# A hand-written order of 1,064 tasks, replaced by another one: split attention and a gated feed-forward block on one core

## The chip, the core and the metric

The kernel runs on one core of one Trainium2 chip. The core has five engines with a queue each: TensorE (PE, with its weight loads shown apart as PEld), VectorE (DVE), ScalarE (ACT), GpSimd (POOL) and SyncE (SP), which in this kernel does nothing but issue transfers. An engine takes its instructions strictly in the order in which they are written; an instruction whose input isn't ready holds up all behind it. The metric is the device time of one execution in microseconds.

## The reference

Four batches (B = 4) of eight heads, 768 positions, 64 numbers per head. Heads 0, 2 and 6 attend causally to all positions. The other five ("streams") see only the first 4 positions and a causal window of 64. The attention's output, laid out as 3072 rows of 512, goes through a gated feed-forward block.

```python
# cut to the core
scores = scale * np.matmul(q, k.transpose(0, 1, 3, 2))
stream_keep = causal & (is_sink | in_win)
mask = np.where(retr[0, :, 0, 0, None, None], full_mask, stream_mask)
a = np.exp(scores - max); a = a / (np.sum(a) + 1e-09); attn = np.matmul(a, v)
x = attn.transpose(0, 2, 1, 3).reshape(B * S, H * D)          # 3072 x 512
g = x @ w_gate                                                # 512 x 1536
out = (g * sigmoid(g) * (x @ w_val)) @ w_out                  # 1536 x 512
```

## The kernel before

**Tiles and tasks.** The sequence is cut into 24 tiles of 128 positions (numbered 0 to 23) in 12 pairs (q0 to q11, k0 to k11 and x0 to x11 are the loads of a pair's q, k and v). Four tiles make a group of 512 rows for the feed-forward block, so there are six groups (g0 to g5). All the work is written as 1,064 tasks, and each is a small function with a name. A name carries its tile or group. The ones that the text speaks of are these:

- `load q3` and the like (L341): a transfer from memory issued by SP into one of 11 raw buffers; a load has to wait until the casts from the buffer's last user are done. `cq`, `ck` (L429) cast q and k to fp16, `cx` (L446) casts v into the table `vt`, `wc g`, `wc v`, `wc o` (L376) cast the weights. For these ACT uses L206, POOL L208 and DVE L212.
- `trq`, `trk` (L469): eight transposes on TensorE for the pairs 0 to 4; `evq`, `evk` (L475) copy them to SBUF. For later pairs SP issues a transposing transfer instead, `dq`, `dk` (L462).
- `sc` (L551, matmuls at L567): scores of a tile in up to four units, each into two PSUM banks. `ex` (L569, L579): the exponential on ACT. `mask` (L581, L587): a product with a mask, on DVE or POOL. `val` (L591, L597): scores times values. `nm` (L600): reciprocal and scaling on DVE, which writes `xb`. `sk`, `sv` (L495, L502): copies of the first four keys and values into each tile's block.
- `xtr` (L609) with `xe` (L624): transposes of a tile's result on TensorE, for tiles 0 to 7; for later ones SP issues `xdma`.
- `gate` and `vals` (L755, matmuls at L759): four matmuls of 512 columns each for one of 12 blocks of the hidden layer; in g0 the blocks 0 to 3 come in halves of 256 columns. `tanh` (L763) on ACT, `stt1` and `stt2` (L767, L773) on DVE.
- The output projection of g0 to g4 uses seven products in place of eight (`out0.p1` to `p7`, L830, matmuls at L839), on sums of blocks of the hidden layer (`hs`, L818, L826) and of the weights (`ws`, L408, L412), each on DVE or POOL. `oe` (L850, L855) gathers the products on DVE or ACT, and `st` (L857) stores them. g5 uses plain matmuls (`out5`, L788, L793).
- `warm` (L315, L321): matmuls that compute nothing. There are ten at the start, and some more groups of fillers between the first transposes.

**What sets the order.** There is no scheduler in the program. Three tables hold what an offline planner chose. `ORDER` is a string of two-digit numbers, the sequence in which the tasks are written into the engines' queues; numbers from 3700 up are warm-ups. `WAYS` has one digit for each task: which of its allowed engines runs it. `SLOTS` has one digit for each buffer taken: which buffer of a ring, and which of the eight PSUM banks. Dependencies are not in the tables; a task's instructions wait by semaphores for what they read and for the former users of their buffers and banks.

```python
for number in P.order():
    if number < P.FILL:
        running.append(P.tasks[number])
        P.tasks[number].run()
    else:
        warm((number - P.FILL) % 16, (number - P.FILL) // 16)
```

Of the kernel before, what the change touches and what calls it, by code (L numbers as in the profile page):

```python
# [13 lines left out]


ORDER = (
    "060004071W1U1V1X0103xz1c1d1ey01f1gzI1i1j092021280A22232B052C2D021hyU1p1q1r1s292A2E2F2L2M0D2X2f2g"
    "2h081Y1b1Z1a1k1l1m1t1u1v0C2W2c2d2e2N2O2S1w2l2m0B24252G2H2I27262P2Q1n2J1o2R1y1z1x2i2j2t2K0F3C3I3J"
    "3K0g0z8o8p0y8e8f8q2U2o2p30310m108h2V8t8j8k8m2k2n8g8i8u8v2x382y0h0E2a2Y118w8x8r8s8l8n13939D9E9F98"
    "999A8y8z902Z2q2r2u2s3334940G3D3L0n14919B9C9596979G9H923M3R3N3S3W3X0k0i161C9h9i9j9c9d9e2z3U3V320H"  # L20
    "3H3G3F3E3O3b9N9O9P9I9J2b353P3637390q1D9f9g9K9k9l3T0o3i3j3f3g179Q9L9R9M3Q3Y3Z3a3c0l1F9r9s9t9m9n9o"
    "3n3o0I3u3l3m0j199S9T9U9X9Y0J3v4344453h3p2v2w3A3B3d3e3k3q3r400p1A9V9W9Z0r1G9p9q4149424A4B464H4748"
    "9u9v9zA13s3t0S0t150N4b4a0M9a9b9yA04N4O4Q4RATB9BABBB4B5B6B7B8BEBFBG0L4P0ZBCBDAd0w1E1M1N1P1O4K4L4M"
    "4C4DAQARASAUAaAbAcAeAfAgAh0x0v0s12ApAqAr4dAO0K3y3z3w3xALAMAiAjANAP0u18BH0XAVAWAX0P0R6vAzB00YB2AY"
    "AZB1B30W1B1K1I4Z4h4gAkAlAmAuAv2T4E4F4Y4e4f0O1H1S1Q1R1T1J1L9wA29xA30c4G4J5D5K5L4I5f5lBIAwA4A6A7A5"
    "ACAA4V4l4m4n4i4j4kA8A9ABADAnAo4v4y4z51505C5I5JAEBMAGAKAF4S4T4U4W4X52AsAtAxAyBLBN0T4q4r4o4p535g5n"
    "5o54AHAIAJBO4s4t4u554w4xBJBPBK56575j5T6KBQ5W5cBX5X5Y4c58596x5A7Q5B7T6z7R707SBZBRBSBTBU5U5VBVBWBY"
    "Ba5s5t5u0a0Q5G5E5F5H5M715N725OBvBsBtBuBwBiBjBk0U6H6JCMCNCOCbCcCd0e81CPCQCWCXCYBlBm5v5w5i5p5q605Z"
    "5a5b5dCeCfCCCDCE5m6364696A6566CHCICJ5rCRCSCFCGCT0V6I6PBxBy5k6y6N5P5Q5R5S67CKCLBz6w73BnBoCACUCVBp"
    "5h5x5y5z62BbBcBdBh68C7C8C2C3616B6C6F6DBqBrC9CBCiCkC4CZCaC0C174BeBf6E6X6YC5C6CjCl6G6U6R6S6M6e6Z6a"  # L30
    "6V6W5eDoDjDkDlDpDqDUDVDWDtDuDrDsDvDADBDwDxDCDmDn0b7P7X7W7O7U6T6b6c6d6fCgCmCh757677Bg7F7G7H7C7L7D"
    "7EDXDYD5D6D788DPDQDRDKDLDDDEDMD8D96L6ODyDzE07I7J7K6gE1E2CnCsCt6Q6h6i6n6o6j6k6l6mDSDT78797A7BDFDG"
    "DHDeDfDg7b7c7d6p6q7Y7j7Z7aDIDJDhDi6r6s6tDZDaDbCoCrCqCp7M7e7f7V7p7q7r7mDNDODcDd7n7o7N6uEmEpEnFLFM"
    "FNFGFHFIFJEcEdEo0d80867g7h7i7k7l8789CuCvEqCyCzE6E8EeCwCxD0D4D1D2D3FKE5E7Ez7x8A8I8J8D8E8F8NFOFP8B"
    "FEFBFCFDFFEwExEyF0EkErEsEtEhEiEjElEuEvE3EAE4E97s7t0f8582838G8WF1F2F3EBEE7u7v7w7z8X8H7yEC8CEFEG8Y"
    "8Z8T8QEX8K8U8L8R8O8M8PEa84F9EYEZF6F7EV8VEHEIEJEK8S8a8b8c8dEfEDEOEbF8FAESETEUEWELENEREMEPEQFTFVGO"
    "GPGQGWGTGUG7GMGCEgGVGXG9GAGBGDGiGjGkGRGSGJGKGLGNGYGZGaGEGFF4F5FpFqFrGHGbGcGGGIGdGeGfFuFvFsFzG0Fx"
    "G2FtFwFyFQFRFXGgGhGlGmG4G5G6FgFYFZG1G3FSFUFeFiFWFaFcG8GnGoGpFbFlFdFfFhFkFoGsGtGuGxFjFmFnGqGrGvGw"
    "GyGzH2H3H0H1H4H7H5H6H8H9"
)  # L40
WAYS = (
    "000010000000000000000000000000000000000000000000000000000000222202201212222202221010000011102210"
    "112200100100000010000000110121212222011000000000000000002100220212011000000000000000200001001000"
    "000201221100011000001001000000000010010010000000011210200010000000000000002000100100000220200110"
    "000000100000000002000010000000000000222200000010000001001000220002020000000100100000010001001000"
    "002102020020000001000000000012000100100000000000110000000000000010000002000001000000001001000001"
    "100000000000022002122100000000000000000100001001000000000000000000000000000000000000000000000000"
    "000000000000000000000000000000000000000000001101000000000000000000000000000000000000000000000000"
    "000000000000000000000000000000001011100010000000000000000000000000000000000000000000000000000000"
    "000000000000000000001010010011000000000000000000000000000000000000000000000000000000000000000000"  # L50
    "000000000110100001000000000000010000000000000000000000000000000000000000000000000000000000000010"
    "111000000000000000001000000000000000000000000000000000000000000000000000000000000000000000000000"
    "00000010"
)
SLOTS = (
    "0015237641826A24867A334524510096788A3905049A38374311A0210016040006142212230223221646560314104140"
    "626231644345614020144616220605456340646213420426144610636540602041626520626443414041046062165222"
    "032434461616520426242614563246106325444261114060612262132061636012442636230612042456120412463601"
    "110301420002121011020041003512510202113212010230020110200131100103213000013001410101124002510051"
    "104021200020030110412312301000011101031025103501111141014010011221012012230001011134102101001021"  # L60
    "500141102110102001101122000430014120110135300021000202140124125310000110110510451041000201004201"
    "4510104111200301151124210311034100202040001001202430120"
)
DIGITS = "0123456789ABCDEFGHIJKLMNOPQRSTUVWXYZabcdefghijklmnopqrstuvwxyz"

# [954 lines left out]
```

## Time and profile before

| | us |
|---|---|
| runs | 248.15, 248.54, 248.74 (median 248.54) |
| the profiled execution | 248.22 |
| its span, first to last instruction | 246.1 |
| TensorE busy | 234.8 |
| VectorE busy | 190.5 |
| ScalarE busy | 148.5 |
| GpSimd busy | 132.7 |

The span is what the profile sees; the execution's own time has about 2.1 us more around it. TensorE's granted clock is full in every slice. Matmuls overlap: the profile gives the time of one from start to end, and in a run of them the next starts earlier than that, so the spacing between starts, and not the mean duration, tells what a series costs. The same holds in a smaller measure for the other engines, whose queued instructions overlap by some 0.05 to 0.1 us.

Transfers: in the first 64 us the loads of 512 KB land one after another, about 1.5 us apart; after that SP mostly waits for the task whose result it is to move.

### The profile page before, as it was taken

The page shows a single profiled execution, that of the slowest core. Times are in us where ns is not written, and L with a number is a line of the kernel's source. Part 1 is how long each engine was busy: PE and PEld are TensorE (multiplying, and loading weights), DVE is VectorE, ACT ScalarE, POOL GpSimd, SP SyncE. Part 2 cuts the span into 40 slices and gives each one's busy share as a digit, 9 for nine tenths or more (in the row PEclk, how much of TensorE's full clock was granted, in tenths as well). Part 3 has the DMA queues.
Part 4 walks back from the last instruction along what each step waited for, and adds up shares of the span by engine and source line. Part 5 has one row for each costly group of instructions (what it writes and reads, how often), then busy time and mean ns, then how long its engine had stood idle before and what let it go on. Part 6 is the DMA issues. An engine that isn't in the chain of part 4 may idle for free.

```text
span 246.1 us, 5624 instructions
## 1 busy us (share of the span) xinstructions
PE 234.8 (95%) x2191; PEld 143.6 (58%) x2191; DVE 190.5 (77%) x326; ACT 148.5 (60%) x236; POOL 132.7 (54%) x137
## 2 busy tenths in 40 slices
PE   7989999999997998999998998999999999999994
PEld 2667755644456777545653645648457664456752
DVE  0769989899998997785889876788698588876920
ACT  5698798877975779869527875653547303321011
POOL 7688697907894585989574063844510802132000
PEclk9999999999999999999999999999999999999999
DMA  6999999999579979992483381632731114000044
GB/s 188 357 346 339 334 353 351 312 310 352 141 221 170 244 159 239 212 243 67 87 164 85 55 159 23 87 86 47 211 92 21 24 21 170 3 0 0 3 170 170
DMA packets 66793, 40.72 MB, mean 165 GB/s; under 512 B 25168, under 2 KB 60240, under 8 KB 66768
## 3 DMA queue, kind: packets, MB, share of 16 engines
q1 hardware_dynamic: 66224, 39.33, 61.8%
q10 hardware_dynamic: 544, 1.05, 1.1%
q8 instruction: 17, 0.28, 0.5%
q14 instruction: 8, 0.07, 0.1%
HBM read 28.31 MB, written 6.29 MB: 141 GB/s over the span
## 4 chain that ended last, share of the span: by engine, by line
PE 75%; DVE 11%; POOL 4%; DMA 3%; issue 3%; SPq 2%; ACT 1%; POOLq 0%; DVEq 0%; ACTq 0%
PE banks L759 38%; PE banks L839 16%; PE banks L567 7%; PE banks L597 5%; PE banks L793 4%; PE banks L321 3%; POOL wt_sb L412 2%; DMA qT<-hq 2%; DVE h_sb L775 2%; PE banks L473 2%; DVE sil L769 2%; DVE xb L605 1%; DVE wt_sb L412 1%; DMA kT<-hq 1%; DVE e L587 1%
## 5 line engine op out<-in xcount | busy, mean ns | idle before, releaser
L579 ACT ACTIVATE e<-banks 128x1024 f16<-128x1024 f32 (+2 forms) x68 | 59.0, 910 | 23.1 <-PE banks L567 15.3
L759 PE MATMUL banks<-xt,wv_sb 128*128 128x512 f16 (+1 forms) x304 | 71.1, 368 | 0.2 <-ACT e L579 0.2
L759 PE MATMUL banks<-xt,wg_sb 128*128 128x512 f16 (+1 forms) x304 | 69.5, 368 | 1.3 <-DVE h_sb L775 0.7
L765 ACT ACTIVATE sig<-banks 128x512 f32<-128x512 f32 (+1 forms) x76 | 43.0, 574 | 43.4 <-PE banks L759 30.2
L587 POOL TENSOR_TENSOR e<-e,m 128x1024 f16<-128x1024 f16 (+1 forms) x25 | 45.9, 1846 | 34.3 <-ACT e L579 34.1
L769 DVE SCALAR_TENSOR_TENSOR sil<-sig,banks 128x512 f32<-128x512 f32 (+1 forms) x76 | 49.2, 657 | 12.9 <-ACT sig L765 10.0
L775 DVE SCALAR_TENSOR_TENSOR h_sb<-sil,banks 128x512 f16<-128x512 f32 (+1 forms) x76 | 49.0, 655 | 5.5 <-PE banks L759 3.8
L759 PEld LDWEIGHTS <-wg_sb 128*128 128x128 f16 x304 | 28.8, 98 | 31.9 <-issue 2.2
L759 PEld LDWEIGHTS <-wv_sb 128*128 128x128 f16 x304 | 28.1, 98 | 29.3 <-issue 1.2
L839 PEld LDWEIGHTS <-h_sb 128*128 128x128 f16 x360 | 34.5, 98 | 8.2 <-DVE wt_sb L412 1.8
L855 DVE TENSOR_TENSOR out_sb<-banks,out_sb 128x512 f32<-128x512 f32 x35 | 23.7, 688 | 6.1 <-PE banks L839 5.5
L826 POOL TENSOR_TENSOR h_sb<-h_sb 128x768 f16<-128x768 f16 x11 | 18.7, 1704 | 15.3 <-DVE hs_sb L826 14.9
L839 PE MATMUL banks<-wt_sb,h_sb 128*128 128x256 f16 x180 | 21.8, 273 | 1.5 <-DVE wt_sb L412 1.5
L567 PE MATMUL banks<-qT,kT 64*128 64x128 f16 x472 | 20.3, 218 | 2.8 <-DVE qT L208 1.0
L839 PE MATMUL banks<-wo_sb,h_sb 128*128 128x256 f16 x180 | 21.9, 273 | 0.0
L567 PEld LDWEIGHTS <-kT 64*128 64x128 f16 x472 | 14.5, 94 | 12.3 <-issue 8.9
L597 PEld LDWEIGHTS <-e 128*128 128x128 f16 x472 | 17.1, 97 | 3.8 <-DVE out_sb L855 0.5
L206 ACT COPY out_sb<-banks 128x512 f32<-128x512 f32 (+1 forms) x9 | 5.1, 574 | 22.2 <-DMA out_dram<-out_sb 14.8
L597 PE MATMUL banks<-vt,e 128*128 128x65 f16 x472 | 18.0, 193 | 0.5 <-POOL vt L208 0.4
L208 POOL CAST vt<-raw 64x512 f16<-64x512 f32 x19 | 11.7, 615 | 10.7 <-DMA raw<-in_v_dram 10.2
L605 DVE TENSOR_TENSOR xb<-banks,rc 128x512 f16<-128x512 f32 x24 | 16.6, 692 | 0.9
L826 POOL TENSOR_TENSOR hs_sb<-h_sb 128x768 f16<-128x768 f16 x5 | 8.2, 1642 | 10.4 <-DVE h_sb L775 8.6
(60 smaller groups left out, 217.7 us busy)
## 6 DMA issues: line engine op xcount, KB each, us to landing
raw<-in_v_dram SPq DMA_DIRECT2D x12, 512.0 KB, 6.6
raw<-in_q_dram SPq DMA_DIRECT2D x8, 512.0 KB, 4.5
raw<-in_k_dram SPq DMA_DIRECT2D x8, 512.0 KB, 5.3
out_dram<-out_sb SPq DMA_DIRECT2D x8, 512.0 KB, 3.3
raw<-in_moe_w_gate_dram SPq DMA_DIRECT2D x6, 512.0 KB, 7.9
raw<-in_moe_w_val_dram SPq DMA_DIRECT2D x6, 512.0 KB, 8.5
raw<-in_moe_w_out_dram SPq DMA_DIRECT2D x6, 512.0 KB, 7.8
raw<-in_q_dram SPq DMA_DIRECT2D x8, 256.0 KB, 6.5
```

The lines of the kernel that those rows point to most:

```text
L567: nc.tensor.matmul(sc[:, c:c + n, :], weights, moving, start=first, stop=last)
L579: nc.scalar.activation(out=to, in_=src, func=AF.Exp, scale=scale)
L587: ENG[task().way].tensor_tensor(out=ev, in0=ev, in1=mm, op=ALU.mult)
L597: nc.tensor.matmul(avs[t][:, odd, n * 66:n * 66 + 65], ee, vv, start=(m == 0), stop=(m == len(bl) - 1))
L605: nc.vector.tensor_tensor(out=xb.rearrange("p n o d -> p o n d"), in0=av[:, :, :, 0:64], in1=rc.to_broadcast([128, 2, 4, 64]), op=ALU.mult)
L759: nc.tensor.matmul(ps, wsb[:, kk, j * 128:(j + 1) * 128], xt[:, kk, c[0]:c[1]], start=(kk == 0), stop=(kk == 3))
L765: nc.scalar.activation(out=sg[g, j, c], in_=gs[g, j, c], func=AF.Tanh, scale=0.5)
L769: nc.vector.scalar_tensor_tensor(out=sl[g, j, c], in0=sg.pop((g, j, c)), scalar=1.0, op0=ALU.add, in1=gs.pop((g, j, c)), op1=ALU.mult)
L775: nc.vector.scalar_tensor_tensor(out=hs[g, j][:, c[0]:c[1]], in0=sl.pop((g, j, c)), scalar=0.5, op0=ALU.mult, in1=vs.pop((g, j, c)), op1=A ...
L826: ENG[T_hs[g, x][part].way].tensor_tensor(out=to, in0=a, in1=b, op=op)
L839: nc.tensor.matmul(rooms[g, p][:, x], left[:, j, 128 * x:128 * x + 128], right[:, j], start=(j == 0), stop=(j == NK - 1))
L855: nc.vector.tensor_tensor(out=cell(*to), in0=rooms[g, p], in1=cell(*other), op=ALU.add)
```

## The change

Only the three tables change. The 1,064 tasks, what they compute, their dependencies, the buffers and the rings are the same. The plan before was made for one chip; the one after was made for the mean over four chips, with durations that were varied and with transfers that land later.

```diff
 ORDER = (
-    "060004071W1U1V1X0103xz1c1d1ey01f1gzI1i1j092021280A22232B052C2D021hyU1p1q1r1s292A2E2F2L2M0D2X2f2g"
...
-    "GyGzH2H3H0H1H4H7H5H6H8H9"
+    "0306071W091U1V1X000A08xy1c0D0C01050B1d1e040gy01f1gzJ1i1h2021282922232B1j1r1s021p1q1w0F2C2D2E2F1b"
...
+    "GzH0H2H3H4H5H7H1H6H8H9"
 )
 WAYS = (
-    "000010000000000000000000000000000000000000000000000000000000222202201212222202221010000011102210"
...
+    "000010000000000000000000000000000000000000000000000000000000221202202202212200200111000111110010"
...
 SLOTS = (
-    "0015237641826A24867A334524510096788A3905049A38374311A0210016040006142212230223221646560314104140"
...
+    "0014237653916A152371476981504A39A2564807049A28352A9168410016041002241601230163620442561014104122"
...
```

Read out, the tables differ in this:

- 120 tasks change their engine and 395 of the chosen buffers and banks are others. Warm-up groups: 3, 4, 4 and 2 before, 2, 4 and 5 after.
- Of the masks 13 ran on DVE and 25 on POOL, now 16 and 22; of the `ws` 7 and 5, now 4 and 8; the `hs` stay 19 and 21 in number, but are dealt otherwise. All `evq` but two go to ACT (two before), most `evk` and `xe` to DVE. Five of the `wc o` are on ACT (three before), none on POOL (two before). Four more stores are issued from ACT.

TensorE's queue up to the first feed-forward matmuls (W and a number: so many warm-ups):

```
before: warm W3 trq0 W4 trk0 W4 sc0.0 trq1 trk1 W2 sc1.0 sc1.1 sc2.0 sc3.0 trk2 val0 val1 trq2 sc3.1 sc4.1
        val2 val3 xtr0 xtr2 xtr1 sc4.0 trq3 gate0.1.0 gate0.0.0 xtr3 sc4.2 sc5.1 vals0.0.0 gate0.1.256
after:  warm W2 trq0 W4 trk0 W5 sc0.0 trq1 trk1 sc1.1 sc1.0 sc2.0 sc3.0 sc3.1 trk2 val1 val0 trq2 val2 sc4.1
        sc4.0 xtr0 xtr1 val3 sc5.1 xtr2 gate0.0.0 gate0.1.0 xtr3 sc4.2 trq3 gate0.1.256
```

ACT's and POOL's queues after, at the places that the text works through (before in brackets where it matters):

```
ACT:  cq0.0 cq0.1 ck0.1 evq0.0 evq0.1 mfill0 evq1.0 ex0.0 ex1.1 ex1.0 sk0.1 ex2.0 ex3.0 ex3.1 cx1.0.1 evq2.0
      evq2.1 ex4.1 ex4.0            [before: mfill0 ck0.1 evq0.0 evk0.0 ex0.0 evk1.0 evk1.1 ex1.0 ex1.1 ...]
POOL: wc g0.1 sk0.2 wc g0.0 mask4.1 mask4.0 wc v0.1 wc g1 ck3 wc v1 mask5.1 cx2.1.1 cx2.0.0 wc g4 mask5.0
      wc v4 mask6.1 sk0.4 wc g2 wc v2 mask6.0 cq4 wc g3 mask7.1 ck4
POOL: ws4.1 ws1.2 ws2.2 ws3.2 hs0.3.0 cx4.0.0 ws2.0 ws3.0 mask9.1 ws4.0 ws4.2 mask10.1 mask11.1 hs1.1.1 mask11.0
      [before: wc o3 ws3.0 ws1.0 sv1.1 cq5 wc o5 ws3.2 ws1.2 ws2.2 hs0.2.1 mask10.0 mask11.0 hs1.1.1 hs1.3.1]
POOL: ck10 hs2.3.0 hs2.2.0 mask20.1 mask19.1   beside DVE: stt1 3.10.0 hs2.2.1 nm16 stt1 3.5.0
```

SP's queue in the middle, after (the loads and transfers that stand behind a wait):

```
... dq6.0 dq6.1 dq7.0 st0.h1 dk7.0 load x10 st0.h0 xdma10 load q9 xdma11 xdma9 load k8 load x6 dk7.1 ...
... xdma13 dq8.0 xdma15 st1.h0 dq10.0 load k10 dk10.1 dk10.0 xdma16 load q11 ...
... dq11.0 xdma17 st2.h1 dk11.0 load x11 xdma20 xdma22 xdma21 xdma23 st3.h1 st5.2.0 st5.3.0 st5.3.1
```

## The prediction

> **What bounds the kernel now.** I read the page first, then the waits, then TensorE's timeline task by task. From the page, the span, the engines' shares and TensorE's row of slices:
>
> ```profile
> span 246.1 us, 5624 instructions
> ...
> PE 234.8 (95%) x2191; PEld 143.6 (58%) x2191; DVE 190.5 (77%) x326; ACT 148.5 (60%) x236; POOL 132.7 (54%) x137
> ...
> PE   7989999999997998999998998999999999999994
> PEclk9999999999999999999999999999999999999999
> ```
>
> TensorE (PE) is the bound: 95%, at full granted clock. The change leaves its work alone, so what can move is time in which it works below its rate. To see that, price its work at the spacing of back-to-back matmuls in the chain that ended last, for example:
>
> ```profile
> 193.78 2.62 PE banks L839 x24
> ...
> 201.59 18.99 PE banks L759 x88
> ```
>
> That is 109 ns for a 256-column matmul of a product and 216 ns for one of 512 columns. In the same way 128 columns take about 57, a score matmul 34, a value matmul 30 and a mark about 110. 544 gate/vals matmuls x 216 = 117.5, 64 short ones x 109 = 7.0, 420 in products x 109 = 45.8, the last output projection 10.4, 472 scores 16.0, 24 marks 2.6, 472 values 14.2, 112 transposes 6.4, 23 warm-ups 5.0: **224.8 us**. TensorE starts at 1.4 and its last matmul ends at 242.8, 3.3 before the end. So 246.1 = 1.4 + 224.8 + 16.6 + 3.3, and 16.6 us are lost inside. Setting each task's start against the running sum gives the places: 2.4 before the first transposes (warm-ups spaced 0.43 instead of 0.216), 4.2 between 6.6 and 32, 6.0 in eight stalls after 73, and about 4 in small steps, mostly 0.1 at each of the 30 turns into score matmuls. Only the 4.2 and the 6.0 belong to the plan.
>
> Three of the late stalls share a cause. The timeline around them (columns: start, us, engine, line, operation):
>
> ```profile
> 75.06 1.64 POOL L826 TENSOR_TENSOR h_sb<-hs_sb,h_sb 128x768 f16<-128x768 f16 x1
> 75.11 2.68 DVE L412 TENSOR_TENSOR wt_sb<-wo_sb,wt_sb 128x512 f16<-128x512 f16 x3 [0.70 <-POOL wt_sb L412]
> 77.84 0.83 PE L839 MATMUL banks<-wt_sb,h_sb 128*128 128x256 f16 x6 [1.55 <-DVE wt_sb L412]
> ...
> 88.92 1.97 POOL L826 TENSOR_TENSOR h_sb<-h_sb 128x768 f16<-128x768 f16 x1
> 89.42 1.88 DVE L826 TENSOR_TENSOR h_sb<-h_sb 128x768 f16<-128x768 f16 x1
> 93.20 0.62 PE L567 MATMUL banks<-qT,kT 64*128 64x128 f16 x16 [0.91 <-DVE xb L605]
> ...
> 130.36 2.12 POOL L587 TENSOR_TENSOR e<-e,m 128x1024 f16<-128x1024 f16 x1 [0.69 <-ACT e L579]
> 130.38 2.51 DVE L826 TENSOR_TENSOR h_sb<-h_sb 128x768 f16<-128x768 f16 x1
> ...
> 229.15 0.55 DVE L826 TENSOR_TENSOR h_sb<-h_sb 128x768 f16<-128x768 f16 x1
> ```
>
> A VectorE (DVE) sum of two SBUF operands takes 0.55 with GpSimd (POOL) idle and 1.88 or 2.51 beside a POOL operation. These blocks led to 1.7 lost at 77.8 (out0.p4), 1.1 at 93.2 (sc13.0) and 0.5 at 134.5 (gate3.1.0). The others: 0.6 at 108.5 (x6 landed at 105.7), 0.4 at 111.0 (dq7.1), 0.6 at 129.7 (a bank), 0.9 at 149.8 (dk8.1), 0.2 at 189.4.
>
> **The change part by part.** Total work per engine, from its mean intervals between queued operations: ACT 136.4 to 137.8, DVE 180.1 to 177.6, POOL 132.0 to 127.7. None nears TensorE, so this alone is worth nothing; only what ends a wait counts.
>
> *Warm-ups.* 13 fillers become 11: 2 x 0.216 = **-0.43**, if nothing else fills the hole.
>
> *Opening, by hand from landings and durations of before.* Loads land about 1.5 us apart and the first four keep their places. q0 is cast on ACT (5.1 to 6.25), the 12 warm-ups end at 1.36 + 12 x 0.427 = 6.5, and sc0.0 starts at 9.34 against 9.22 (five fillers before it instead of four). mfill0 (2.25 on ACT, in cover at 4.3 before) now stands behind evq0.1: ACT is free again at 10.5, ex0.0 ends at 12.2, ex1.1 at 13.1, ex1.0 at 14.05, ex2.0 at 15.3, ex3.0 at 16.2. Banks hang on these, so sc3.1 loses 0.2 and val0.1 0.4; val2.1 waits for cx1.0.1 on ACT until 17.7 (0.75). In exchange evk1, evk2, xe0 and xe1 moved to DVE, and sc4.1, which lost 1.05 to DVE's evq2, starts at 18.2, after val2. gate0.0.0 starts at 20.2 (21.7 before), gate0.1.256 waits for v0's cast and xe3 until 22.6, trk3 ends near 28.5. Lost since the first transposes: 3.0 to 3.3 against 4.2. I take **-0.9**; bounds -1.6 and +0.5, for landings that shift by one place (1.5).
>
> *POOL from 19 to 46.* It now has sk0.2, mask4.0, mask4.1 and sk0.4 among its casts. At sc7.0 TensorE has done 29.2 us of its work and needs POOL's first 29.3; before, 31.2 and 27.4: 3.9 us of lead gone. Chained: cx2.0.0 ends at 29.7, then g4 30.75, mask5.0 32.85, v4 33.9, mask6.1 35.3, sk0.4 35.75, g2 36.8, v2 37.8, mask6.0 39.9, g3 42.0. sc7.1, gate0.4.0 and trq4 want their inputs at 35.7, 36.8 and 41.2: no slack. I take **+0.4**; bounds 0 and +2.
>
> *Weight sums and g0's products.* Before, POOL reached o5 at 70.5 behind q5's cast, and ws4.0 on DVE ran into hs0.2.1. Now all o casts but o3's are on ACT, the last near 64.8; POOL runs ws1.2, ws2.2, ws3.2 (3 x 1.13 from 62), hs0.3.0 1.64, cx4.0.0, ws2.0, ws3.0, mask9.1 1.4, ws4.0, ws4.2 to 73.7. out0.p7 comes near 74.1 and needs ws3.0 at 70.0; out0.p4 near 76.1 and needs ws4.2. The 1.7 goes. If POOL is over 2.4 late it is back. **-1.4**.
>
> *sc13.0.* g1's sums are nearly all on DVE now (hs1.2.1, hs1.3.0, hs1.2.0 after nm10), with POOL in mask11.0 until 85; nm10 ends near 87.6, sc11.3 wants it at 88.1. **-0.9**.
>
> *Landings.* SP's queue is re-ordered. dq6, dk7.0, st0.h0, xdma10, xdma11 and xdma9 chain on nm11 (92.1): xdma9 lands near 96.3, gate2.2.0 wants it at 97.2. What queues behind xdma9 is k8, x6, dk7.1; x6 lands near 101.7, its casts end at 104.8, val13 wants them at 105.5. st1.h0 now stands ahead of dq10.0, load k10 and dk10, and waits for oe1.c12 (120): k10 lands at 128, its cast ends at 129, dk10.0 lands at 133; sc20.1, nine gate/vals tasks earlier than before, wants it at 136.8. st2.h1 stands ahead of dk11.0: 161.7 against sc22.1 at 166. These have 0.7 to 4 of slack; of the 1.9 that before lost to landings I take **-1.2**; bounds -1.9 and +1.5.
>
> *New tight places.* hs2.2.1 on DVE (near 130) meets POOL's hs2.3.0 and hs2.2.0, and nm16 and sc18.0 queue behind it: up to 1.2. mask10.0 on DVE meets mask10.1 on POOL: 0.3. vals4.10.0 waits for a bank behind sv3.2 and tanh4.11.0 on ACT: 0.2. hs4.1 to hs4.4 run on POOL alone, hs4.2.1 to 213.3 where out4.p6 wants it at 213.9: 0 to 0.5. Two more turns into scores: 0.2. **+1.4**. Stores moved to ACT issue in 0.37 each behind their data; oe5.0.0 behind oe5.1.0 still frees its bank 0.7 before out5.3.0, so the end stays at 3.3.
>
> *Where rule and row differ.* The group rows price DVE's masks at 0.78 and 0.66 us, its ws at 0.71: three masks in, three ws out, +0.1 on an engine with room. The Trainium skill, "SBUF — State Buffer", section "Who interferes with whom", says that a DVE instruction with two SBUF inputs contends with a GpSimd one that reads SBUF, and that the second to start blocks fully. The single rows above agree with it. Such operations on DVE stay 39 (13 masks, 19 hs, 7 ws become 16, 19, 4); six blocks cost DVE about 8 us, and 3.3 reached TensorE. By the mean rows the collisions removed are gain; by the rule they are dealt anew. I side half-way with the rule: of the 2.3 taken above for out0.p4 and sc13.0, plus gate3.1.0's 0.5, I put back **+0.6** beyond hs2.2.1.
>
> Sum: -0.43 - 0.9 + 0.4 - 1.4 - 0.9 - 1.2 + 1.4 + 0.6 = -2.4; with gate3.1.0 and gate3.9.0 (1.1 together), whose partners moved, half gone: **-3.0**. The profiled execution took 248.2 (span 246.1 and 2.1 around it), the median of the runs is 248.5: 248.5 - 3.0 = **245.5**.
>
> **The rivals.** *The early POOL chain sets the pace*: 1.5 to 2 us behind by 46, paid in full since nothing after it has TensorE waiting on purpose. For it: the zero slack, POOL busy without a break from 19. Against: its loads land before their turns. 245.5 + 2 = 247.5. *Stalls only change places*: before had a plan too and still lost 10; the 39 collisions and the landings cost the same again, and only the opening's sign is open: 248.5. *Slower, by blocked sums*: DVE's hs2.2.1, hs3.2.0, hs3.2.1 or a mask meets a POOL sum of 1.64 or mask of 2.1 where norm (nm) is next in DVE's queue, so that scores and SP's transposes behind nm are late. Each costs TensorE up to about 1.7 (the most seen); the saving of 3.0 is used up by two such stalls more than I count, and with three or four the time is 250.5. For it: the plan's collisions are as many as before. Against: the g0 and g1 sums, which cost most, are moved apart.
>
> **How the numbers follow.** The forecast 0.50 (its own range 243.8 to 247.0: the bounds of opening and landings), the POOL chain 0.16, places only 0.08, slower 0.26. Less than 0.2% (0.5 us) can't be told from no change. Faster: 0.50 + 0.16 less 0.02 = 0.64; within: 0.09; slower: 0.27. Eight in ten: from 243.3 to 250.3, which leaves out the lowest tenth of the forecast and the upper half of the slower case.
>
> **What would show it.** Right: gate0.0.0 near 20, out0.p4 with no wait for wt_sb, the waits for xb before sc13.0 gone, products of g2 after hs2.2.1 the largest new wait, TensorE's last matmul near 239.8. Wrong: a TensorE wait of over 1 us for POOL's wg_sb or kT between 33 and 46; a DVE sum of over 1.5 us ahead of nm or a product; waits for landed transposes at sc20.1, sc22.1 or gate2.2.0; a lower granted clock.

## The result, and the profile after

The changed kernel takes **245.74 us** (median of 245.54 to 246.15) where the kernel before takes 248.64 beside it: a ratio of 0.988, 95% interval 0.985 to 0.991, or 2.9 us less (2.1 to 3.8). The forecast was 245.5 and 3.0 us less. Below, "the profiled execution after" is the one of 246.15, the slowest of the four, and the one before is of 248.22; 2.07 of the 2.9 can be followed in this pair.

The page of the changed kernel, with the rows that were shown of before (span, engines, TensorE's slices and granted clock):

```profile
span 244.4 us, 5604 instructions
...
PE 234.5 (96%) x2189; PEld 143.6 (59%) x2189; DVE 186.7 (76%) x324; ACT 148.5 (61%) x235; POOL 129.0 (53%) x140
...
PE   7989999998999999799999999999999999999995
PEclk9999999999999999999999999999999999999999
```

TensorE is the bound as before, at full clock. Its work is 0.43 less (two warm-ups). The row of the clock does not show the slow start that the prediction read from the warm-ups: in both kernels the first ones are 0.43 us apart and the later ones 0.22. Behind the opening, which looks the same, the four dents of the old row of slices have become two: an 8 at slice 10 (55 to 61 us) and a 7 at slice 17 (98 to 104). What they hold is in the waits of TensorE (columns: what was waited for, us in total, times, longest):

```profile
PE banks L759 <- DMA xt<-xb: 1.4, 1, 1.4
PE banks L321 <- POOL ident L234: 1.4, 1, 1.4
PE banks L759 <- DVE sil L769: 1.1, 3, 0.4
PE banks L567 <- DVE xb L605: 1.0, 2, 0.5
PE banks L597 <- POOL vt L208: 0.7, 1, 0.7
PE banks L839 <- DVE out_sb L855: 0.6, 2, 0.4
```

The row for `wt_sb`, 1.55 us before, is gone. In its place there is one landing (`xt`) of 1.4 and seven shorter waits for DVE. A stall costs 0.1 to 0.2 more than such a wait says, since queued matmuls overlap and those on both sides of a stall do not; "lost" below is counted from start to start, and "waited" is the profile's figure. The timeline of the changed kernel around five places (columns: start, us, engine, line, operation, and in brackets the idle time before it and who ended it):

```profile
56.28 2.12 POOL L587 TENSOR_TENSOR e<-e,m 128x1024 f16<-128x1024 f16 x1 [0.69 <-ACT e L579]
57.59 1.36 DVE L587 TENSOR_TENSOR e<-e,m 128x1024 f16<-128x1024 f16 x1
...
77.70 2.79 PE L839 MATMUL banks<-wt_sb,h_sb 128*128 128x256 f16 x24
78.68 1.39 POOL L587 TENSOR_TENSOR e<-e,m 128x640 f16<-128x640 f16 x1 [1.45 <-ACT e L579]
78.75 1.75 DVE L826 TENSOR_TENSOR h_sb<-h_sb 128x768 f16<-128x768 f16 x1
...
101.24 1.02 PE L759 MATMUL banks<-xt,wg_sb 128*128 128x512 f16 x4 [1.36 <-DMA xt<-xb]
...
133.79 1.64 POOL L826 TENSOR_TENSOR h_sb<-h_sb 128x768 f16<-128x768 f16 x1
134.57 1.28 DVE L826 TENSOR_TENSOR h_sb<-hs_sb,h_sb 128x768 f16<-128x768 f16 x1
136.75 0.85 PE L567 MATMUL banks<-qT,kT 64*128 64x128 f16 x24 [0.51 <-DVE xb L605]
...
186.25 1.64 POOL L826 TENSOR_TENSOR h_sb<-h_sb 128x768 f16<-128x768 f16 x1 [2.93 <-DVE h_sb L826]
186.68 1.61 DVE L826 TENSOR_TENSOR h_sb<-hs_sb,h_sb 128x768 f16<-128x768 f16 x1
188.95 1.47 PE L839 MATMUL banks<-wt_sb,h_sb 128*128 128x256 f16 x12 [0.45 <-DVE out_sb L855]
```

The matmuls at 77.70 (out0.p4 and out0.p6) follow without a gap: the old 1.7 is gone. But DVE's sums and masks still run beside POOL's, at other places: 1.36, 1.75, 1.28 and 1.61 for operations that take 0.55 (a sum) or 0.67 (this mask) undisturbed. Summed over all of DVE's masks, `hs` and `ws`, the time beyond what they take undisturbed was 7.9 us in 6 operations before and is 6.4 us in 10 now.

Where the time went is best seen in one number: by how much TensorE starts the same work earlier than in the kernel before, after about so many us of that work (each task's start against the running sum that the prediction used; the first column counts the warm-ups, the differences leave them out). Each column is one profiled execution. The last two are two of the experiments, which start from the changed kernel.

| work done | about where in the changed kernel | changed | six moves (e8) | best (e10) |
|---|---|---|---|---|
| 23 us | val4.1, end of the opening | 1.27 | 0.69 | 1.28 |
| 42 | sc8.1 | 1.22 | 0.63 | 1.23 |
| 62 | gate1.0.0 | 0.39 | 0.58 | 1.18 |
| 86 | out1.p7 | 2.00 | 2.56 | 3.16 |
| 100 | vals2.7.0 | 1.35 | 2.16 | 3.86 |
| 121 | gate3.5.0 | 2.26 | 3.05 | 4.64 |
| 150 | out2.p3 | 2.41 | 3.78 | 5.37 |
| 172 | vals4.8.0 | 2.62 | 3.99 | 5.59 |
| 190 | vals5.7.0 | 1.34 | 3.58 | 5.18 |
| end | last matmul | 1.44 | 3.68 | 5.28 |

For the changed kernel 0.3 more comes behind the last matmul (3.0 in place of 3.3) and 0.35 outside the span (1.75 in place of 2.1), which makes the 2.07. These two parts are no accident of one execution: all executions of the changed kernel and of its variants have 1.74 to 1.87 outside the span, all of the kernel before 2.07 to 2.18.

The gain of TensorE does not grow evenly. It is made in the opening, between 62 and 86 and around 121, and given back three times: 0.8 at gate1.1.0 and vals1.2.0, 0.65 at gate2.2.0, 1.3 at out3.p6 and vals4.0.0. e8's column is 0.58 lower from the opening on, ahead of all its moves: in that execution the warm-ups stayed 0.43 apart to the last of the first twelve, and the eight transposes of trq0 took 1.02, where in the changed kernel's execution the last two came 0.28 and 0.22 apart and trq0 took 0.67.

### The profile page after: what moved, and what is told of

Read it like the earlier page. It is cut to its first block, busy times and chain, and to the rows that moved or that the text cites. A ratio compares the mean times of both kernels' runs of the same rounds, so it can differ in the third digit from the quotient of the medians.

```text
span 244.4 us, 5604 instructions
## 1 busy us (share of the span) xinstructions
PE 234.5 (96%) x2189; PEld 143.6 (59%) x2189; DVE 186.7 (76%) x324; ACT 148.5 (61%) x235; POOL 129.0 (53%) x140
## 3 DMA queue, kind: packets, MB, share of 16 engines
q10 hardware_dynamic: 1376, 2.62, 2.9%
## 4 chain that ended last, share of the span: by engine, by line
PE 54%; DVE 19%; issue 8%; DMA 6%; POOL 5%; SPq 5%; ACT 2%; DVEq 0%; POOLq 0%
PE banks L759 34%; PE banks L839 10%; PE banks L793 4%; DMA raw<-in_moe_w_val_dram 4%; DVE h_sb L775 4%; PE banks L567 3%; DVE h_sb L826 3%; SPq L349 3%; DVE sil L769 3%; PE banks L597 2%; POOL hs_sb L826 2%; DVE out_sb L855 2%; DVE xb L605 2%; DMA xt<-xb 2%; DVE e L587 2%
## 5 line engine op out<-in xcount | busy, mean ns | idle before, releaser
L759 PE MATMUL banks<-xt,wg_sb 128*128 128x512 f16 (+1 forms) x304 | 70.3, 368 | 1.9 <-DMA xt<-xb 1.4
L587 POOL TENSOR_TENSOR e<-e,m 128x640 f16<-128x640 f16 (+1 forms) x22 | 37.8, 1727 | 27.2 <-ACT e L579 24.3
L759 PEld LDWEIGHTS <-wg_sb 128*128 128x128 f16 x304 | 28.5, 98 | 30.7 <-issue 3.1
L826 POOL TENSOR_TENSOR hs_sb<-h_sb 128x768 f16<-128x768 f16 x7 | 11.5, 1640 | 40.9 <-DVE h_sb L775 29.4
L826 POOL TENSOR_TENSOR h_sb<-h_sb 128x768 f16<-128x768 f16 x11 | 18.0, 1639 | 8.2 <-PE banks L839 4.4
L597 PE MATMUL banks<-vt,e 128*128 128x65 f16 x472 | 18.2, 193 | 1.0 <-POOL vt L208 0.7
L208 POOL CAST vt<-raw 64x512 f16<-64x512 f32 x22 | 14.4, 654 | 4.8 <-DMA raw<-in_v_dram 2.3
L206 ACT COPY out_sb<-banks 128x512 f32<-128x512 f32 (+1 forms) x7 | 4.0, 570 | 19.1 <-PE banks L793 16.0
```

Of the source, the lines that this page charges most:

```text
L587: ENG[task().way].tensor_tensor(out=ev, in0=ev, in1=mm, op=ALU.mult)
L597: nc.tensor.matmul(avs[t][:, odd, n * 66:n * 66 + 65], ee, vv, start=(m == 0), stop=(m == len(bl) - 1))
L759: nc.tensor.matmul(ps, wsb[:, kk, j * 128:(j + 1) * 128], xt[:, kk, c[0]:c[1]], start=(kk == 0), stop=(kk == 3))
L826: ENG[T_hs[g, x][part].way].tensor_tensor(out=to, in0=a, in1=b, op=op)
```

## The experiments

The theory was that single stalls were taken out (opening, out0.p4, parts of sc13.0 and of the landings), that each is worth about its length, and that part came back as new collisions. The rival was that stalls only change places: whatever is taken out at one place is waited for at the next. Each diff below shows the queues as they read; in the code only digits of `ORDER` and `WAYS` (and `SLOTS` where two plans are joined) change.

**Two plans joined (e1, e2).** The front of the new plan with the rest of the old one, cut at places where no buffer is claimed ahead of its former users.

```diff
-ORDER of before
+ORDER of after up to xe7 (e1) or up to sk2.3 (e2), then what is left, in the order of before
 (WAYS and SLOTS of each task from the plan that it stands in)
```

> The kernel before, with its first 277 tasks (everything up to xe7, the first 50 us) taken from the changed kernel in order, engines and buffers, and the rest in the old order. Theory, from the two traces: at the end of this stretch the changed kernel had lost 8.1 us against its running sum of work and the kernel before 8.9, and it has two fillers (0.43) less; the later stalls of before (out0.p4 1.7, sc13.0 1.1 and so on) stay. So -1.2, with 0.3 either way. By the prediction's steps (fillers -0.43, opening -0.9, POOL chain +0.4): -0.9. Rival, later stages swallow it because they wait for transfers: 0 to -0.4.

> The same with the first 664 tasks (up to sk2.3, the first 126 us) from the changed kernel. Theory, from the traces: by there the changed kernel has lost 13.5 against 14.4, and 0.43 of fillers, so -1.4; the stretch from 50 to 126 adds next to nothing, since the removed stalls (1.7 and 1.1) came back as gate2.2.0 1.5, sc11.3 0.6, gate1.1.0 0.6 and vals1.2.0 0.4. By the prediction's steps (opening, POOL chain, weight sums, sc13.0, most of the landings, mask10.0): about -2.9. Rival, the late part carries the gain: above -0.7.

Measured: e1 250.88 against 249.05, ratio 1.0085 (1.0067 to 1.0103), 2.1 us slower; e2 250.16, 1.0049 (1.0022 to 1.0076), 1.2 slower. Neither theory came true, nor e1's rival. e2's rival (above -0.7) fits the number only because a loss lies above -0.7 too: a front that loses 1.2 doesn't show that the late part carries the gain. The seams cost more than the fronts had gained. TensorE's timeline in e1:

```profile
51.28 1.02 PE L759 MATMUL banks<-xt,wv_sb 128*128 128x512 f16 x4 [0.89 <-DVE xt L208]
54.59 0.46 PE L567 MATMUL banks<-qT,kT 64*128 64x128 f16 x9 [0.49 <-DVE kT L212]
66.56 0.81 PE L759 MATMUL banks<-xt,wv_sb 128*128 128x512 f16 x3 [1.36 <-DVE h_sb L775]
```

All three waits behind the seam are for DVE's copies and products. A reading that fits is that the new plan had put off what the old one expects to be done there. So the joined plans do not divide the gain between stages; they show that at these two seams a stage's gain was not to be had without the stage behind it.

e2 also showed something that none of the prediction's views held. TensorE at its seam, first the timeline, then the windows of 2 us (us, then busy time and instructions of PE, PEld, DVE, ACT and POOL, granted clock, DMA share, GB/s):

```profile
135.89 1.87 PE L759 MATMUL banks<-xt,wg_sb 128*128 128x512 f16 x4 [2.66 <-DVE sil L769]
```

```profile
134.00:136.00 2.00, 0.11 (x1) 0.10 (x1) 1.87 (x4) 0.67 (x2) 0.29 (x1) 0.97 0.00 0
136.00:138.00 2.00, 2.00 (x6) 0.63 (x5) 1.90 (x3) 0.73 (x2) 0.00 (x0) 0.50 0.00 0
138.00:140.00 2.00, 2.00 (x8) 0.82 (x7) 0.56 (x2) 1.43 (x2) 0.00 (x0) 0.68 0.00 0
140.00:142.00 2.00, 2.00 (x38) 1.77 (x37) 1.86 (x5) 0.93 (x2) 0.00 (x0) 1.00 0.39 67
```

After a stall of 2.66 us the granted clock is 0.50 for 3.4 us (from 135.87 to 139.28): four matmuls take 1.87 in place of 1.02, and at half rate 3.4 us lose 1.7, so a stall of 2.7 costs about 4.4. Five of e2's six runs have a mean clock of 0.993 and take 249.7 to 251.0; the sixth has 1.0 and takes 248.8. The Trainium skill, "TensorE: Matmul & The Clock Gate", section "What's actually happening", has the array fall to half rate after an idle window of about 3.4 us that runs by itself; here a stall shorter than that was enough. The traces tell more. In e2, e4 and e5 every stretch of one clock lasts a multiple of 3.41 us. Once at full rate, the clock fell 16 times ahead of the last matmul, and in the 3.41 us ahead of each fall TensorE was busy, as the profile has it, for 0.00 to 0.48 of the time. Of all other stretches of 3.41 us on that grid, in all traces, one (of those at full rate) was as low as 0.43 (e5, 60.65 to 64.07), and the next ones 0.51 and 0.52. Two stretches of e4, the first followed by a fall, the second not (us, then PE's busy time and instructions, granted clock, DMA share, GB/s):

```profile
12.84:16.25 3.41, 1.65 (x25) 1.00 1.11 334
169.87:173.28 3.41, 1.77 (x9) 1.00 0.56 96
```

So, but for that one, the share of busy time in such a stretch tells the falls from the rest, and the length of one stall does not: a stall of 1.25 lies across the end of the first stretch, one of 2.24 across the end of the second. No stall of the kernel before (at most 1.55) or after (1.36) was followed by a fall; the lowest stretch of the kernel before, around out0.p4, was at 0.55, near the edge, and that of the kernel after at 0.66.

**One collision taken out of the kernel before (e3).**

```diff
-POOL: ... ws1.2 ws2.2 hs0.2.1 mask10.0 ...      DVE: ws4.2 ws2.0 ws4.0 hs0.2.0 nm8
+POOL: ... ws1.2 ws2.2 mask10.0 ...              DVE: ws4.2 ws2.0 ws4.0 hs0.2.0 hs0.2.1 nm8
```

> The kernel before with one task on another engine: hs0.2.1, the sum of h_sb that ran on POOL at 75.06 beside DVE's weight sum, goes to DVE. Theory (the blocked weight sum is the cause of the 1.7 lost at out0.p4): ws4.2 then takes 0.42 in place of 1.88, out0.p4 starts 1.3 to 1.6 earlier, DVE has 0.55 more to do just behind it: -1.2, between -0.8 and -1.6. Rival, the stall only moves on (nm8 or the sums for out0.p6 become late): -0.3 to +0.3.

Measured: 249.07 against 249.05, ratio 1.0007 (0.9990 to 1.0024). The timeline of e3 (DVE's weight sums, then what follows on DVE, POOL and PE):

```profile
75.22 1.22 DVE L412 TENSOR_TENSOR wt_sb<-wo_sb,wt_sb 128x512 f16<-128x512 f16 x3 [0.71 <-POOL wt_sb L412]
76.49 2.79 PE L839 MATMUL banks<-wt_sb,h_sb 128*128 128x256 f16 x24
...
87.62 1.65 POOL L826 TENSOR_TENSOR h_sb<-h_sb 128x768 f16<-128x768 f16 x1
87.69 1.99 DVE L826 TENSOR_TENSOR hs_sb<-h_sb 128x768 f16<-128x768 f16 x1
92.17 0.62 PE L567 MATMUL banks<-qT,kT 64*128 64x128 f16 x16 [1.01 <-DVE xb L605]
98.66 1.16 PE L839 MATMUL banks<-wt_sb,h_sb 128*128 128x256 f16 x9 [0.62 <-POOL h_sb L826]
100.95 1.02 PE L759 MATMUL banks<-xt,wv_sb 128*128 128x512 f16 x4 [0.48 <-DVE out_sb L855]
102.63 3.61 PE L759 MATMUL banks<-xt,wg_sb 128*128 128x512 f16 x16 [0.65 <-DVE out_sb L855]
```

The theory is right about the cause: the three weight sums take 1.22 in place of 2.68, and out0.p4 starts at 76.49 in place of 77.84. It is wrong about the worth. The sums of g1 meet again at 87.6, now with another DVE sum as the loser, and three waits that the kernel before didn't have (0.62, 0.48 and 0.65, at out1.p6, vals2.2.0 and gate2.2.0) come by 103. At sc13.0 TensorE is 1.03 ahead of the kernel before, at gate2.2.0 1.25 behind: more than the gain is gone. Not all of that comes from the moved sum. Two of the waits hang on one store that landed late in this execution: DVE's oe1.c11 waited 2.65 and began at 100.21, behind the landing of st0.h0 at 100.09 (98.13 before), and vals2.2.0 and gate2.2.0 take over the banks that oe1.c11 and, behind it, oe1.r6 read. In e6 below, which has the old plan here, landings were late too (xdma11 at 101.33, 100.39 before), and vals2.2.0 waited 0.80. Measured against e6 instead, TensorE goes from about 1.5 ahead at out0.p4 to 0.3 behind at gate2.2.0. So the rival holds: the gain of one removed stall is gone 26 us later.

**The two fillers alone (e6).**

```diff
-PE: ... sc0.0 trq1 trk1 W2 sc1.0 sc1.1 ...
+PE: ... sc0.0 trq1 trk1 sc1.0 sc1.1 ...
```

> The kernel before without the two warm-up matmuls ahead of sc1.0 (13 fillers become 11, as in the changed kernel). Theory: -0.43, what two 216 ns matmuls take, since sc1.0 waits for nothing there. Rival, the opening is set by what lands and is cast (q2, x1, the first weights), and sc4.1 or gate0.1.256 waits so much longer: 0, within 0.15.

Measured: 249.0 against 249.05, ratio 1.0000 (0.9981 to 1.0019). TensorE's timeline in e6:

```profile
17.68 0.40 PE L567 MATMUL banks<-qT,kT 64*128 64x128 f16 x8 [0.99 <-DVE qT L208]
25.59 1.12 PE L759 MATMUL banks<-xt,wv_sb 128*128 128x256 f16 x8 [0.41 <-DVE sil L769]
```

sc4.1 starts 0.45 earlier than in the kernel before, xtr3 0.04 earlier, and gate0.9.0 0.1 later. The hole is filled by 23 us, where the first `gate` tasks wait for weights: load g0 landed at 20.02 before and at 20.13 here, and wc g0.0 ended at 21.58. In the changed kernel g0 is loaded ahead of q3 and landed at 18.68; its gate0.0.0 starts at 20.53 and not at 21.69. The earlier load is the likely reason; no run moved it alone.

**Tables swapped (e4, e5).**

```diff
-ORDER, SLOTS of before, WAYS of before
+ORDER, SLOTS of before, WAYS of after          (e4)
+ORDER, SLOTS of after,  WAYS of before         (e5)
```

> The kernel before with the changed kernel's engines (WAYS) and its own order and banks. Theory, after what grafts and single moves showed (a plan's parts only fit each other): slower than before, by 1 to 6, since the 120 tasks that changed their engine now stand at places in their queues that were chosen for other engines. Rival, the choice of engines carries the gain by itself (fewer sums and casts on POOL): 1 to 3 faster.

> The changed kernel's order and banks with the old engines (WAYS). Theory: slower than before, by 1 to 8, as above. Rival, the order carries the gain by itself: 1 to 3 faster.

Measured: e4 292.0 against 248.9, ratio 1.174 (1.171 to 1.178); e5 301.5, ratio 1.212 (1.207 to 1.217). The sign was right, the size off by ten. The first waits of TensorE in e4:

```profile
PE banks L759 <- DVE sil L769: 5.6, 4, 4.8
PE banks L597 <- DVE e L587: 4.7, 3, 2.2
PE banks L597 <- ACT vt L206: 4.5, 3, 1.8
PE banks L597 <- POOL vt L208: 3.9, 1, 3.9
```

The engines have about as much to do (DVE 188.9, POOL 129.9 and ACT 149.9 in e4 against 190.5, 132.7 and 148.5 before), and the tasks are the same. A task that stands at its place for one engine holds up, on another, a queue that was timed without it; the mean granted clock falls to 0.953 and 0.942. What the 120 engine changes are worth inside the span depends on the order that they stand in.

One part goes with the engines alone. Outside the span e4 has 1.79 to 1.85 us and 2.99 behind the last matmul, like the changed kernel (1.74 to 1.87 and 3.0); e5 has 2.21 to 2.24 and 3.29, like the kernel before (2.07 to 2.18 and 3.3). So some 0.6 of the 2.9 us comes with the new choice of engines, whatever the order, and lies behind TensorE's work. Which of the 120 changes does it, the stores issued from ACT or another, no run shows.

**The changed kernel's own stalls (e7, e8, e9).** Beside them the changed kernel was run again on the same chip as the control.

> The changed kernel itself, again, on the same chip as the three variants of it and the kernel before: 0.988 of the kernel before, between 0.985 and 0.991, so 246.0 where the kernel before takes 249.0.

Measured: 246.22 against 248.98, ratio 0.9886 (0.9857 to 0.9914). e7 changes SP's queue alone:

```diff
-SP: dq7.0 st0.h1 dk7.0 load x10 st0.h0 xdma10 load q9 xdma11 xdma9 load k8
+SP: dq7.0 st0.h1 xdma9 dk7.0 load x10 st0.h0 xdma10 xdma11 load q9 load k8
```

> The changed kernel with two transfers moved in SP's queue alone: xdma9 (its data, nm9, was ready at 86.4, it was issued at 96.4) goes up to just behind st0.h1, and load q9 goes down behind xdma11. Theory (gate2.2.0's 1.48 is the order of SP's queue, not a late result): xdma9 lands near 92, xdma11 near 98, gate2.2.0 starts at 99.8 in place of 101.2; if nothing behind is tight, -1.4 against the changed kernel. What the first four experiments showed speaks for less: stalls that go are found again at the next tight place (x6 for val13, then nm16 and sc18.0). I expect -0.7, between 0 and -1.4. Rival, PE waits for DVE's and POOL's results there in any case: 0, within 0.2.

Measured: 245.01, ratio 0.9848 (0.9811 to 0.9884), 1.2 less than the control; three runs at 244.9 to 245.0, one at 246.3, and the profiled one at 247.8. In that one the landing is gone (xdma9 landed at 91.7, xdma11 at 99.6) and two others stand in its place:

```profile
99.38 1.47 PE L839 MATMUL banks<-wt_sb,h_sb 128*128 128x256 f16 x12 [1.35 <-DVE out_sb L855]
...
106.19 1.02 PE L759 MATMUL banks<-xt,wg_sb 128*128 128x512 f16 x4 [1.23 <-DVE sil L769]
```

The first is the store st0.h0, which now stands behind xdma9: it landed at 98.54 (95.61 in the changed kernel), and its output buffer is what DVE's oe1.r6 waited 1.50 for. Behind the second, hs1.4.0 on DVE started at 103.49, 0.14 behind mask14.1 on POOL, and took 1.68. This execution is the slowest of the five; what the faster ones gained by is not profiled. e8 changes DVE's queue, with one store behind it:

```diff
-DVE: hs0.1.1 hs0.3.1 cx4.0.1 stt1 1.9.0 stt2 1.9.0 sk1.3 mask8.0 stt1 1.1.0 stt2 1.1.0
+DVE: hs0.1.1 hs0.3.1 stt1 1.9.0 stt2 1.9.0 cx4.0.1 sk1.3 stt1 1.1.0 mask8.0 stt2 1.1.0
-DVE: hs1.3.1 oe0.c12 nm10 sv1.4                      SP: st0.h0 xdma10
+DVE: hs1.3.1 nm10 oe0.c12 sv1.4                      SP: xdma10 st0.h0
-DVE: stt1 3.10.0 hs2.2.1 nm16 stt1 3.5.0 stt2 3.5.0
+DVE: stt1 3.10.0 nm16 stt1 3.5.0 stt2 3.5.0 hs2.2.1
-DVE: hs3.2.0 oe3.r1 hs3.2.1 oe3.c11 nm22 sv3.4 stt1 4.7.0
+DVE: hs3.2.0 oe3.r1 oe3.c11 hs3.2.1 nm22 stt1 4.7.0 sv3.4
```

> The changed kernel with six moves in DVE's queue (one of them takes st0.h0 behind xdma10 on SP): results that TensorE waits for go ahead of sums, masks and copies that it doesn't need yet. They aim at gate1.1.0 0.62, vals1.2.0 0.42, sc11.3 0.61, sc18.0 0.67, out3.p6 0.61 and vals4.0.0 0.62, together 3.5. Theory (these stalls are DVE's order behind blocked sums): at least half of it stays, -1.8, between -1.0 and -3.0 against the changed kernel. Rival, stalls only change places, as in the kernel before with one sum moved: 0, within 0.4.

Measured: 243.88, ratio 0.9795 (0.9762 to 0.9827), **2.3 less than the control**. TensorE's waits in e8, whose rows for `sil` and `xb` are gone:

```profile
PE banks L321 <- POOL ident L234: 1.4, 1, 1.4
PE banks L759 <- DVE out_sb L855: 1.1, 1, 1.1
PE banks L597 <- DVE rc L604: 0.7, 1, 0.7
PE banks L597 <- ACT e L579: 0.3, 1, 0.3
```

The row with `out_sb` is gate2.2.0 at 100.43, 0.14 behind xdma9's landing at 100.29: the release that the profile names had long been done. So of the 3.5 aimed at, 2.3 stayed, and the rival fails. The table above shows it place by place: e8's lead over the changed kernel grows by 0.78 between 42 and 62 us of work (gate1.1.0, vals1.2.0), by 0.37 up to 86 (sc11.3), by 0.58 between 121 and 150 (sc18.0) and by 0.87 between 172 and 190 (out3.p6, vals4.0.0). The edit suggests why: the moves put what TensorE waits for ahead of what may be late, so that a block holds up something that nobody needs yet. Besides, two of the ten blocks went and a third became shorter (hs3.2.1, 0.89 in place of 1.61); 4.2 us in 8 are left. The six moves were not run one by one. Both at once (e9) was to show whether they add:

> The changed kernel with the moves of both others. If the stalls of SP's queue and of DVE's queue are separate, the gains add: -2.5 against the changed kernel, between -1.4 and -4.2. If there is one chain, no more than the larger of the two.

Measured: 245.51 median, ratio 0.9808 (0.9756 to 0.9860), with runs from 242.3 to 246.2, so widely spread that they don't settle it. The profiled execution, of 243.75, shows one of the causes (DVE, POOL, then PE):

```profile
100.95 1.75 DVE L826 TENSOR_TENSOR h_sb<-h_sb 128x768 f16<-128x768 f16 x1
```

```profile
100.89 1.39 POOL L587 TENSOR_TENSOR e<-e,m 128x640 f16<-128x640 f16 x1 [7.29 <-ACT e L579]
```

```profile
103.72 1.02 PE L759 MATMUL banks<-xt,wg_sb 128*128 128x512 f16 x4 [1.23 <-DVE sil L769]
```

With no landing to wait for, TensorE is early enough that mask14.1 starts on POOL at 100.89, 0.06 ahead of hs1.4.0 on DVE. In the changed kernel hs1.4.0 came first (101.31 against 101.83) and took 0.55.

**A version better than both (e10), and a test of that cause (e11).**

```diff
 the moves of e8, and
-SP: st0.h1 dk7.0 load x10 xdma10 st0.h0 load q9 xdma11 xdma9 load k8
+SP: st0.h1 dk7.0 load x10 xdma10 st0.h0 xdma9 xdma11 load q9 load k8
 e11, besides:
-DVE: oe1.c22 hs1.4.0 sk2.2 stt1 2.2.0 ... stt2 2.8.0 stt2 2.0.0 nm13
+DVE: oe1.c22 sk2.2 stt1 2.2.0 ... stt2 2.8.0 stt2 2.0.0 hs1.4.0 nm13
```

> The changed kernel with the six moves in DVE's queue, xdma9 up to just behind st0.h0 (so that the store is as early as with the six moves alone, where it landed at 94.95) and load q9 behind xdma11. Theory, from the run with both: the landing was gone, but TensorE came so early that mask14.1 started on POOL at 100.89, just ahead of hs1.4.0 on DVE at 100.95, which took 1.75 in place of 0.55, and gate2.6.0 waited 1.23 for what stood behind it. That is still so here: gate2.2.0 without a wait, gate2.6.0 with 1.0 to 1.4, 243.5 where the kernel before takes 249.0, no more than 0.5 better than the six moves alone (0.9795 of the kernel before). Rival, the wait at gate2.6.0 has another cause, the transfers that moved: then it is gone here, 242.3.

> The same with one more move: hs1.4.0 goes down in DVE's queue behind stt2 2.0.0, away from mask14.1. Theory (a blocked sum is what ate the landing's gain): gate2.6.0 starts without a wait and 1.2 more is kept: 242.4, between 241.8 and 243.2, where the kernel before takes 249.0 (0.9735). Rival, hs1.4.0 meets another POOL operation where it now stands, or nm13 behind it comes late: no gain over the run without this move.

Measured: e10 **242.38** against 248.9 (242.17 to 243.08), ratio 0.976 (0.974 to 0.979), so 6.5 us less by the medians and 5.9 by the ratio; e11 242.64, ratio 0.977 (0.975 to 0.979). The timeline of e10, DVE and then POOL:

```profile
100.42 0.55 DVE L826 TENSOR_TENSOR h_sb<-h_sb 128x768 f16<-128x768 f16 x1
```

```profile
100.67 1.55 POOL L587 TENSOR_TENSOR e<-e,m 128x640 f16<-128x640 f16 x1 [7.16 <-ACT e L579]
```

For e10 the theory's forecast (a wait at gate2.6.0 of 1.0 to 1.4) failed, and the rival's number came true for a cause of the theory's: hs1.4.0 now starts 0.25 ahead of the mask instead of 0.06 behind, takes 0.55, and gate2.6.0 waits for nothing. The Trainium skill, "SBUF — State Buffer", section "Who interferes with whom", says that the order of issue decides who blocks; this pair is it, with 1.2 us of DVE's time hanging on 0.3. For e11 the rival held: the sum, moved on, meets the next POOL mask (mask12.0, 106.72 to 108.85) at 108.14, takes 1.12, and sc15.2 waits 0.40 behind nm13:

```profile
108.14 1.12 DVE L826 TENSOR_TENSOR h_sb<-h_sb 128x768 f16<-128x768 f16 x1
```

The store st0.h0 landed at 95.06 in e10 and at 96.00 in e9, where oe1.r6 was ready for it. That may be why most of e9's runs are slower than e10's; it is not shown, since only one execution of e9 left a trace.

## Why the prediction came out right

The sum was right (-3.0 forecast, -2.9 measured), and in part by luck: the errors of its steps cancel, and some 0.6 of the 2.9 came from where it had forecast nothing. By its steps:

- **Warm-ups (-0.43), opening (-0.9).** Together right: TensorE is 1.27 ahead at the end of the opening, forecast 1.33. The walk by landings was good to 0.4 us at the places that count (sc4.1 at 18.35 for 18.2, gate0.0.0 at 20.53 for 20.2, trk3's end at 28.8 for 28.5). The split was wrong: e6 shows that fewer fillers give nothing by themselves, since "if nothing else fills the hole" was the condition, and weights not yet landed fill it.
- **POOL chain (+0.4).** Too dear: 0.05 is lost up to sc8, with one small loss of 0.21 (gate0.11.0). No slack was not the same as late.
- **Missed: +0.83 between 42 and 62.** gate1.1.0 and vals1.2.0 lost 0.62 and 0.42 behind DVE's hs0.1.1 (1.38) and mask8.0 (1.36). The re-dealt collisions (+0.6) covered it in size, not in place.
- **Weight sums, sc13.0 (-1.4, -0.9).** From 62 to 86 the gain is 1.61; the steps, with +0.3 for the meeting with mask10.1, gave 2.0. out0.p4's wait is gone as forecast, but narrowly: POOL's ws4.2 ended at 77.23 and not at 73.7, later by 3.5, where the prediction had named 2.4 as too much. The wait stayed away because out0.p4 came late as well (77.70 for 76.1). The size of the new wait there was right (0.34 lost at out0.p5 for 0.3), though it was hs0.4.1 and not mask10.0 that met mask10.1. The waits for `xb` before sc13.0 were not gone: sc11.3 in front of it lost 0.61, since nm10 stands behind oe0.c12 and two slowed sums.
- **Landings (-1.2).** The step that failed most: about -0.4 in this execution (of the 1.9 that the kernel before had lost, 1.48 came back at gate2.2.0). The walk had xdma9 land near 96.3 and gate2.2.0 want it at 97.2; it landed at 101.10 and was wanted at 99.8. nm11 ended at 95.1, not 92.1, and behind load q9 (landed 99.34) xdma11 took 5.5 from issue to landing. That xdma9 has been ready since 86.4 and stands behind xdma11 was in the queue to be seen. e7 confirms the place. How much it costs varies: in the profiled execution of the control xdma9 landed at 100.53, gate2.2.0 waited 0.72 and lost 0.84, which would make the step -1.1.
- **hs2.2.1 (up to 1.2), gate3.9.0 and gate3.1.0 (half of 1.1 gone).** Right in kind: the old two are wholly gone (0.9 gained from 100 to 121), sc18.0 lost 0.67 behind hs2.2.1's 1.28 and nm16.
- **The slower rival, in part.** hs3.2.1 meeting a POOL sum was its mechanism by name, and it cost 1.3 at out3.p6 and vals4.0.0. One such stall more than counted wasn't enough to turn the sign; two were its threshold.
- **The end.** Forecast unchanged, in fact about 0.3 less behind the last matmul and 0.3 less outside the span, in all executions of the changed kernel. By e4 and e5 this goes with the choice of engines, which the prediction had priced at nothing here. Without it TensorE gained 2.3 where 3.0 had been forecast.

Of the signs named for being right, two held (gate0.0.0 near 20, out0.p4 without a wait) and three did not: sc11.3 still waited for `xb` ahead of sc13.0, the largest new wait was the landing at gate2.2.0 and not behind hs2.2.1, and TensorE's last matmul ended at 241.4 (240.9 in the control) for 239.8, for the most part because of the late give-back. Of the signs named for being wrong, two came true: DVE sums of over 1.5 us ahead of a norm or a product (hs0.4.1 1.75, hs3.2.1 1.61) and the wait for a landing at gate2.2.0.

The experiments say how far stalls can be added up. Single edits of the old plan (e3, e6) kept nothing of the 1.35 and 0.45 that they gained on the spot, and the joined plans (e1, e2) lost. The prediction's terms were therefore not independent savings; they were a reading of one whole plan against another, place by place. That the sum came out because each place had been walked in its new surroundings is a reading and not shown; the errors that cancel speak for luck as well. That the new plan gains because it was made for varied durations is not shown by any run: e8 and e10, ordered by hand from one trace, gain more. e8 takes 2.3 us less than the changed kernel on the same chip. e10 ran on another chip, without the changed kernel beside it; by its gain over the kernel before it is 3.1 (ratios) to 3.8 us (medians) better.

## What to carry to other kernels

Where TensorE is at 95% in a hand-ordered kernel, price a stall only together with what is next: ask which result arrives next with little slack, since a local gain of 1.35 us was returned in full within 26 us. The moves that kept their gain put results that TensorE waits for ahead of sums, masks and casts that can be late, in DVE's queue and in SP's; added to the new plan, which had taken 2.9 us off, they brought it to 6.5 (5.9 by the ratio) on the chip that they ran on. Choose engines and order together: here the engines of one plan with the order of the other cost 43 and 53 us. Look also behind the last matmul and outside the span: 0.6 us lay there.

## What the hardware showed that was not expected

- A stall of TensorE of 2.66 us was followed by 3.4 us at a granted clock of 0.50, so that it cost about 4.4 in all. All 16 falls in e2, e4 and e5 followed 3.41 us in which TensorE was busy less than half of the time (at most 0.48); a single stall of 2.24 us in a busier stretch (0.52, e4) was not followed by one.
- 0.3 us decide a collision. hs1.4.0 took 0.55 when it started 0.25 ahead of POOL's mask (which then took 1.55 for 1.39) and 1.75 when it started 0.06 behind.
- Not only POOL's sums and masks slow a DVE sum: hs1.3.1 took 0.96 in the changed kernel beside a POOL cast (cx8.1.1), against 0.55.
- A transposing transfer issued behind the load of 512 KB took 5.5 us to land (xdma11 in the changed kernel, 95.15 to 100.62), and 3.3 with the load behind it (e10, 94.27 to 97.54). Other transfers ahead of it differ too, so the load is not shown to be the only reason.
- The time outside the span differs by 0.3 us between the two choices of engines (1.74 to 1.87 against 2.07 to 2.24), with either order.
